# Transform pieces ahead of the layers: a Fourier mixing and a two-layer network woven into one stream of matmuls

## The chip, the cores and the metric

One core of a Trainium2 chip runs the whole kernel in one launch. The metric is the time of the launch on the device, in microseconds; the time given for a kernel is the median of its runs.

## The reference

```python
def _attn_ref(x, filt_r, filt_i):            # x: (8, 3008, 256), filters: (1505, 256)
    X = np.fft.rfft(x, axis=1)
    F = (filt_r + 1j * filt_i)[None, :, :]
    Y = X * F
    return np.fft.irfft(Y, n=x.shape[1], axis=1).astype(np.float32)

def _moe_ref(x, w_in, w_out, alpha):         # x: (24064, 256), w_in: (256, 2048), w_out: (2048, 256)
    h = x @ w_in
    g = np.maximum(h, 0.0) + alpha * np.minimum(h, 0.0)
    return (g @ w_out).astype(np.float32)
```

Each of 8 batches of 3008 tokens is filtered along its tokens in the frequency domain, and all 24064 tokens then go through two layers with a leaky step between them.

## The kernel before

The Fourier transform of length 3008 is split into 47 x 64 and done with small matrices, in stages that the code calls pieces. `piece_a` is the first stage (16 pieces a batch): a matmul of 512 columns on `xs`, which ScalarE moves out of the accumulator into `asb`. `save_a` writes a quarter of `asb` to memory, and `turn_a` reads it back with the axes exchanged into `at`. `piece_b` is a forward pair (12 a batch): two matmuls, and two VectorE products with the filter, `ww` and `uu`, that read the accumulator; GpSimd then sends `ww` with its halves exchanged to `sw` by two transfers. `piece_s` adds `sw` to `uu` on VectorE. `piece_c` is the inverse stage (12): matmuls on `uu`, moved out to `v` by ScalarE; in the batch of index 1 there is no `piece_s`, and `piece_c` takes four matmuls, on `uu` and `sw`. `turn_c` writes `v` to memory and, after the last quarter, reads `zt` back. `piece_d` is the last stage (16): four small matmuls on `zt`, moved out to `yT`, which the layers read.

Batch 0 is done by a class of its own, `First`, ahead of everything; its last 12 turns (`piece_t`) and last-stage pieces are left for the first steps of the layers.

The layers run over 48 blocks of tokens (512 each, one in twelve of 384). A block has 16 steps. In step j, `up(j)` multiplies 128 columns of the first weights with the block's tokens (two matmuls, L414); in odd steps ScalarE moves two steps' results together to `gtb` (L420), and VectorE applies the leaky step (two L423, one L424). `down(j)` does a sixteenth of the second layer of the block before (four matmuls, L433); at its steps 7 and 15 ScalarE moves a result to `osb` (L438), and SyncE's queue stores it.

The order on each engine is the order in which the program is written. A dictionary, `plan`, holds for each step a list of pieces, put there by `put(step, fn, *args)`. In the main loop a step writes `up(j)`, then `down(j)` of the block before, then the pieces of that step in the order in which they were put. Six blocks, 96 steps, pass while one batch goes through the layers; `plan_fft` spreads the pieces of batch index b over the steps before its tokens are needed. Its arguments are the step of the first `piece_a` and their spacing (`a0`, `ga`), the step of `turn_a` (`ta`), the first `piece_b` and the spacing (`b0`, `gap`), the distance to `piece_s` and `piece_c` (`add`, `lag`), and the first `piece_d` (`d0`). A batch's first stage overlaps the forward and inverse stages of the batch before it.

The accumulator memory has 8 banks: the layers' first results `hps` take two buffers of two banks, the second layer's `op` two, and all transform pieces share the last two, the buffers `psF`. A piece can start when one of these two has been emptied, by ScalarE (a, c, d), or by VectorE's two products (b).

Of the kernel before, what the change touches and what calls it, by code (L numbers as in the profile page):

```python
# [64 lines left out]
def kernel(  # L65
# [59 lines left out]
    def load_x(b, c):  # L125
        xs = p_x.tile([2 * N1, 8 * D], FP16, name="xs")
        for h in range(2):
            nc.gpsimd.dma_start(out=xs[h * N1 : h * N1 + N1], in_=xrow(b, h, c))  # L128
        return xs
# [113 lines left out]
    both = (on_act, on_dve)  # L243
# [198 lines left out]
    plan = {}  # L442

    def put(step, fn, *args):
        plan.setdefault(step, []).append((fn, args))

    def plan_fft(b, a0, ga, ta, b0, gap, add, lag, d0, quarters=1, x_late=False):
        f = Fft(b)
        for i in range(16):
            put(a0 + ga * i, f.piece_a, i, on_act)  # L450
        for c in range(4):
            put(a0 + ga * (4 * c + 3), f.save_a, c)
            if b + 1 < NB:
                put(int(b0 + gap * c) + 1 if x_late else a0 + ga * (4 * c + 3) + 1,
                    lambda b=b, c=c: xc.update({(b + 1, c): load_x(b + 1, c)}))
        for q in range(quarters):
            w = NK1 // quarters
            put(ta, f.turn_a, nc.sync, w * q, w * q + w)
        for kp in range(12):
            put(int(b0 + gap * kp), f.piece_b, kp)  # L460
            if add:
                put(int(b0 + gap * kp) + add, f.piece_s, kp)
            put(int(b0 + gap * kp) + lag, f.piece_c, kp, on_act)
        for q in range(4):
            put(int(b0 + gap * (3 * q + 2)) + lag + 1, f.turn_c, q)
        for i in range(16):
            put(d0 + min(i, 4) + 2 * max(i - 4, 0), f.piece_d, i, on_act)

    for g, t0, d0, gap, evs in ((1, 0, 4, 1, both), (2, 17, 24, 2, (on_dve,)), (3, 32, 40, 2, (on_act,))):
        for i in range(4):  # L470
            put(t0 + gap * i, f0.piece_t, 4 * g + i, evs[i % len(evs)])
            put(d0 + gap * i, f0.piece_d, 4 * g + i, evs[i % len(evs)])
# [4 lines left out]
    for i in range(4):  # L477
        put(17 + 3 * i, neg, 6 * i, 6 * i + 6)
    put(29, lambda: nc.gpsimd.dma_start(out=filt_s[64:128], in_=filt_s[0:64]))
    plan_fft(1, 16, 1, 32, 44, 2.5, 0, 6, 92, 4)  # L480
    plan_fft(2, 66, 2, 97, 110, 4.5, 8, 13, 187, 4, True)
    for b in range(3, NB):
        p = 96 * (b - 1)
        plan_fft(b, p - 62, 2, p - 27, p + 6, 5, 8, 13, p + 91, 1, True)

    prev = None
    step = 0
    for p, t0, tn, _ in blocks:
        blk = Block(p, t0, tn)
        for j in range(16):  # L490
            blk.up(j)
            if prev is not None:
                prev.down(j)
            for fn, args in plan.pop(step, ()):
                fn(*args)
            step += 1
        prev = blk
    for q in range(16):
# [32 lines left out]
```

## Time and profile before

| | |
|---|---|
| median of 3 runs | 805.74 us (804.57 to 806.27) |
| the profiled execution's own time | 805.14 us |
| its span, first to last instruction | 803.4 us |
| TensorE matmuls busy | 779.2 us (97%) |
| TensorE weight loads busy | 539.9 us (67%) |
| VectorE busy | 646.5 us (80%) |
| ScalarE busy | 595.6 us (74%) |
| GpSimd busy | 139.9 us (17%) |
| moved by transfers | 100.59 MB, 125 GB/s on average |
| granted TensorE clock | 0.999 |

The times of the runs are of the whole launch; the span is that of one profiled execution. Matmuls overlap in the records, so a busy TensorE need not be one at full speed: the distance from one start to the next tells that. A bracket behind a row of the timeline is the time in which the engine stood idle just before it, and what ended that.

### The profile page before, as it was taken

Reading aid. Unit: us, or ns where it says so; the run is one execution under the profiler, and the core shown is the slowest. Engines: PE = TensorE matmul, PEld = TensorE weight load, DVE = VectorE, ACT = ScalarE, POOL = GpSimd, SP = SyncE. Lnnn points to the kernel's source line nnn. Section 1 sums busy time; section 2 is a strip of 40 time slices with the busy share of each in tenths; the row PEclk is TensorE's granted clock in tenths of the full one; section 3 lists DMA queues with packets and bytes.
Section 4 is the critical chain, followed back from the end, with each engine's and each line's share of the span. In section 5 each row is a group of like instructions: output and inputs, shape, how many; then the busy total and the mean of one; then the engine's idle time right before and its main releaser. Section 6 shows DMA issues by size and latency. Waiting matters only on the chain.

```text
span 803.4 us, 16151 instructions
## 1 busy us (share of the span) xinstructions
PE 779.2 (97%) x5980; PEld 539.9 (67%) x5980; DVE 646.5 (80%) x1449; ACT 595.6 (74%) x836; POOL 139.9 (17%) x269
## 2 busy tenths in 40 slices
PE   6989999999999999999999999999999999999997
PEld 5756667666667666776667766766666766776665
DVE  4797886698878987798877988789877899777773
ACT  3677668878777787777867787687877776686663
POOL 7511230042103210041201321032100122000000
PEclk9999999999999999999999999999999999999999
DMA  9968546474574447464483644845475134511111
GB/s 182 209 135 186 138 109 201 140 155 127 142 180 102 109 112 184 138 119 125 118 198 91 142 115 118 215 93 112 112 180 143 47 89 103 135 40 31 40 40 53
DMA packets 94247, 100.59 MB, mean 125 GB/s; under 512 B 11320, under 2 KB 81992, under 8 KB 94040
## 3 DMA queue, kind: packets, MB, share of 16 engines
q1 hardware_dynamic: 79512, 68.80, 31.8%
q0 software_dynamic: 14656, 30.75, 20.1%
q8 instruction: 47, 0.77, 0.4%
q14 instruction: 32, 0.26, 0.1%
HBM read 56.26 MB, written 46.66 MB: 128 GB/s over the span
## 4 chain that ended last, share of the span: by engine, by line
PE 88%; DVE 6%; ACT 4%; issue 1%; DMA 1%; POOL 0%; ACTq 0%; DVEq 0%; POOLq 0%
PE op L433 38%; PE hps L414 37%; PE psF L164 3%; PE psF L231 3%; PE psF L209 2%; PE psF L184 2%; ACT gtb L420 2%; DVE gtb L424 2%; DVE m L423 1%; DMA xs<-in_x_dram 1%; DVE ww L188 1%; DVE uu L189 1%; PE hps L281 1%; ACT v L238 1%; ACT osb L438 0%
## 5 line engine op out<-in xcount | busy, mean ns | idle before, releaser
L420 ACT ACTIVATE gtb<-hps 128x1024 f16<-128x1024 f32 (+1 forms) x384 | 384.9, 1003 | 115.1 <-PE hps L414 113.9
L433 PE MATMUL op<-wout_s,gtb 128*128 128x256 f16 x3008 | 451.1, 272 | 0.6 <-DVE gtb L424 0.6
L414 PE MATMUL hps<-yT,win_s 128*128 128x512 f16 (+1 forms) x1536 | 449.5, 374 | 1.9 <-ACT yT L238 1.5
L433 PEld LDWEIGHTS <-gtb 128*128 128x128 f16 x3008 | 293.2, 98 | 190.8 <-DVE m L423 1.4
L423 DVE TENSOR_SCALAR m<-gtb,alm_s 128x512 f16<-128x512 f16 (+1 forms) x768 | 237.7, 351 | 108.4 <-ACT gtb L420 107.0
L424 DVE TENSOR_TENSOR gtb<-gtb,m 128x1024 f16<-128x1024 f16 (+1 forms) x384 | 261.6, 681 | 22.7
L191 POOL DMA_DIRECT2D sw<-ww x168 | 87.7, 527 | 499.1 <-DVE ww L188 488.2
L414 PEld LDWEIGHTS <-win_s 128*128 128x128 f16 x1536 | 145.4, 98 | 34.0 <-issue 6.2
L238 ACT ACTIVATE asb<-psF 96x512 f16<-96x512 f32 x112 | 66.4, 593 | 34.6 <-PE psF L164 33.9
L238 ACT ACTIVATE yT<-psF 128x376 f16<-128x376 f32 x120 | 58.0, 483 | 10.7 <-PE psF L231 10.6
L238 ACT ACTIVATE v<-psF 128x512 f16<-128x512 f32 x84 | 50.1, 596 | 16.5 <-PE psF L209 16.4
L438 ACT ACTIVATE osb<-op 128x512 f32<-128x512 f32 x96 | 56.1, 584 | 6.1 <-issue 3.2
L188 DVE TENSOR_TENSOR ww<-psF,filts_s 128x512 f16<-128x512 f32 x84 | 57.4, 684 | 0.3 <-PE psF L184 0.3
L189 DVE TENSOR_TENSOR uu<-psF,filt_s 128x512 f16<-128x512 f32 x84 | 57.2, 681 | 0.0
L164 PE MATMUL psF<-xs,wf_s 94*96 94x512 f16 x112 | 43.2, 386 | 5.9 <-ACT v L238 2.7
L231 PE MATMUL psF<-wi_s,zt 96*128 96x94 f16 x504 | 42.1, 204 | 1.8 <-DVE zt L241 1.2
L128 POOL DMA_DIRECT2D xs<-in_x_dram x64 | 34.4, 547 | 35.5 <-PE psF L164 23.2
L231 PEld LDWEIGHTS <-zt 96*128 96x128 f16 x512 | 35.6, 97 | 6.5 <-issue 2.0
L209 PE MATMUL psF<-uu,twi_s 128*128 128x256 f16 x168 | 33.4, 273 | 0.0
L184 PE MATMUL psF<-at,twf_s 128*128 128x256 f16 x168 | 32.1, 272 | 1.1 <-ACT yT L238 0.9
L196 DVE TENSOR_TENSOR uu<-uu,sw 128x512 f16<-128x512 f16 x72 | 30.1, 418 | 0.0
L209 PEld LDWEIGHTS <-twi_s 128*128 128x128 f16 x192 | 18.5, 98 | 2.1
(57 smaller groups left out, 192.5 us busy)
## 6 DMA issues: line engine op xcount, KB each, us to landing
out_dram<-osb SPq DMA_DIRECT2D x128, 128.0 KB
xs<-in_x_dram POOLq DMA_DIRECT2D x64, 188.0 KB, 4.6
a_dram<-asb SPq DMA_DIRECT2D x28, 384.0 KB
sw<-ww POOLq DMA_DIRECT2D x168, 64.0 KB, 2.1
v_dram<-v SPq DMA_DIRECT2D x112, 96.0 KB
zt<-v_dram SPq DMA_DIRECT2D x28, 384.0 KB
at<-a_dram SPq DMA_DIRECT2D x20, 384.0 KB
at<-a_dram SPq DMA_DIRECT2D x32, 96.0 KB
```

What stands on the lines that cost most here:

```text
L164: nc.tensor.matmul(ps[0:96], wf1_s, xs[:, o : o + 512], start=True, stop=True)
L188: nc.vector.tensor_mul(ww, px, filts_s[:, 2 * kp : 2 * kp + 2])
L189: nc.vector.tensor_mul(uu, px, filt_s[:, 2 * kp : 2 * kp + 2])
L191: nc.gpsimd.dma_start(out=sw[o : o + 64], in_=ww[64 - o : 128 - o])
L209: nc.tensor.matmul(pv[:, kh], twi_s[:, k1], u[:, kh], start=u is us[0], stop=u is us[-1])
L231: nc.tensor.matmul(ps[:, m], self.zt[:, 8 * g + 4 * mh + m, dh * 128 : dh * 128 + 128], wi3_s, start=True, stop=True)
L238: nc.scalar.activation(o, i, AF.Copy)
L414: nc.tensor.matmul(self.hps[:, j % 2, 0:tn], win_s[:, kt, j * 128 : (j + 1) * 128], yT[:, kt, self.t0 : self.t0 + tn], start=(kt == 0), st ...
L420: nc.scalar.activation(g[:, :, 0:tn], self.hps[:, :, 0:tn], AF.Copy)
L423: nc.vector.tensor_scalar(m[:, i, 0:tn], g[:, i, 0:tn], 0.0, a, OP.min, OP.mult)
L424: nc.vector.tensor_add(g[:, :, 0:tn], g[:, :, 0:tn], m[:, :, 0:tn])
L433: nc.tensor.matmul(self.op[:, si % 2], self.gts[k][:, 128 * si : 128 * si + 128], wout_s[:, k], start=(k == 0), stop=(k == 15))
```

## The change

Four things change, all in the order of the same instructions.

1. In each step the pieces are written ahead of `up(j)` and `down(j)`, not behind them.
2. `piece_b` is put at `b0` plus an even number wherever `piece_s` is used (index 2 on), and `b0` is odd there: `p + 5` in place of `p + 6`, 109 in place of 110. So these forward pairs stand in odd steps; `piece_s`, `piece_c` and `turn_c` follow at the old distances.
3. From index 3 on the first stage begins at `p - 70` with a spacing of 2.5 steps, 40 steps in all; it began at `p - 62` with a spacing of 2.
4. The steps of the loads of the next batch's x are given as a list. For the batch of index 2 (the third) the last two of the four loads move from steps 28 and 32 to 73 and 74.

Besides, the last-stage pieces of batch 0 that begin at steps 4 and 24 begin at 6 and 25.

```diff
-    def plan_fft(b, a0, ga, ta, b0, gap, add, lag, d0, quarters=1, x_late=False):
+    def plan_fft(b, a0, ga, ta, b0, gap, add, lag, d0, quarters, x_at):
         f = Fft(b)
         for i in range(16):
-            put(a0 + ga * i, f.piece_a, i, on_act)
+            put(int(a0 + ga * i), f.piece_a, i, on_act)
         for c in range(4):
-            put(a0 + ga * (4 * c + 3), f.save_a, c)
+            put(int(a0 + ga * (4 * c + 3)), f.save_a, c)
             if b + 1 < NB:
-                put(int(b0 + gap * c) + 1 if x_late else a0 + ga * (4 * c + 3) + 1,
+                put(x_at[c],
                     lambda b=b, c=c: xc.update({(b + 1, c): load_x(b + 1, c)}))
...
+        bs = [b0 + (2 * int(gap * kp / 2) if add else int(gap * kp)) for kp in range(12)]
         for kp in range(12):
-            put(int(b0 + gap * kp), f.piece_b, kp)
+            put(bs[kp], f.piece_b, kp)
             if add:
-                put(int(b0 + gap * kp) + add, f.piece_s, kp)
-            put(int(b0 + gap * kp) + lag, f.piece_c, kp, on_act)
+                put(bs[kp] + add, f.piece_s, kp)
+            put(bs[kp] + lag, f.piece_c, kp, on_act)
         for q in range(4):
-            put(int(b0 + gap * (3 * q + 2)) + lag + 1, f.turn_c, q)
+            put(bs[3 * q + 2] + lag + 1, f.turn_c, q)
...
-    for g, t0, d0, gap, evs in ((1, 0, 4, 1, both), (2, 17, 24, 2, (on_dve,)), (3, 32, 40, 2, (on_act,))):
+    for g, t0, d0, gap, evs in ((1, 0, 6, 1, both), (2, 17, 25, 2, (on_dve,)), (3, 32, 40, 2, (on_act,))):
...
-    plan_fft(1, 16, 1, 32, 44, 2.5, 0, 6, 92, 4)
-    plan_fft(2, 66, 2, 97, 110, 4.5, 8, 13, 187, 4, True)
+    plan_fft(1, 16, 1, 32, 44, 2.5, 0, 6, 92, 4, (20, 24, 73, 74))
+    plan_fft(2, 66, 2, 97, 109, 4.5, 8, 13, 187, 4, (110, 114, 118, 122))
     for b in range(3, NB):
         p = 96 * (b - 1)
-        plan_fft(b, p - 62, 2, p - 27, p + 6, 5, 8, 13, p + 91, 1, True)
+        plan_fft(b, p - 70, 2.5, p - 27, p + 5, 5, 8, 13, p + 91, 1, (p + 6, p + 10, p + 16, p + 20))
...
         for j in range(16):
+            for fn, args in plan.pop(step, ()):
+                fn(*args)
             blk.up(j)
             if prev is not None:
                 prev.down(j)
-            for fn, args in plan.pop(step, ()):
-                fn(*args)
             step += 1
```

## The prediction

> **What bounds the kernel now.** I read the page first, then the timeline of TensorE, then the waits of single stretches, then VectorE and ScalarE around each wait.
>
> ```profile
> span 803.4 us, 16151 instructions
> PE 779.2 (97%) x5980; PEld 539.9 (67%) x5980; DVE 646.5 (80%) x1449; ACT 595.6 (74%) x836; POOL 139.9 (17%) x269
> ```
>
> TensorE is the bound by its busy share. Whether that busy time is also full speed is read from the starts:
>
> ```profile
> 401.10 0.59 PE L414 MATMUL hps<-yT,win_s 128*128 128x512 f16 x2
> 401.53 0.60 PE L433 MATMUL op<-wout_s,gtb 128*128 128x256 f16 x4
> 401.96 0.59 PE L414 MATMUL hps<-yT,win_s 128*128 128x512 f16 x2
> ```
>
> Two matmuls of 512 columns take 0.43 us, four of 256 columns 0.43 us: a step is 0.87 us, and outside a few places every step in the timeline has just this length. The order of matmuls can win nothing there. What is left to win are the places where TensorE stands. After the first block those taken up below come to some 12 us, and nearly all are of one kind: a transform piece waits for one of the two psF banks. The timeline of one such place, the last of its window (two rows), and the row of the waits of 352 to 420 us:
>
> ```profile
> 363.68 0.38 PE L184 MATMUL psF<-at,twf_s 128*128 128x256 f16 x2
> 364.50 0.61 DVE L423 TENSOR_SCALAR m<-gtb,alm_s 128x512 f16<-128x512 f16 x2 [0.16 <-ACT gtb L420]
> 365.75 0.68 DVE L188 TENSOR_TENSOR ww<-psF,filts_s 128x512 f16<-128x512 f32 x1
> 366.36 0.68 DVE L189 TENSOR_TENSOR uu<-psF,filt_s 128x512 f16<-128x512 f32 x1
> 366.50 0.38 PE L209 MATMUL psF<-uu,twi_s 128*128 128x256 f16 x2
> 367.09 0.42 PE L164 MATMUL psF<-xs,wf_s 94*96 94x512 f16 x1 [0.21 <-DVE uu L189]
> 367.35 0.38 PE L414 MATMUL hps<-yT,win_s 128*128 128x512 f16 x1
> 399.55 0.38 PE L209 MATMUL psF<-uu,twi_s 128*128 128x256 f16 x2
> 400.23 0.60 PE L414 MATMUL hps<-yT,win_s 128*128 128x512 f16 x2
> ```
>
> ```profile
> PEld L164 <- DVE uu L189: 1.6, 4, 0.5
> ```
>
> The forward pair (L184) of an odd step ends up behind that step's own layer pair on VectorE: the pair's L423 starts at 364.50, ww only at 365.75, and the bank is free at 367.04, 3.36 us after its matmuls began. Three steps on an inverse piece (L209) takes the other bank, and the first-stage piece (L164) of the next batch stands. From c to the next layer matmul should be 0.43 us and is 0.85: 0.42 lost, twice what the bracket says. Each window in which two batches overlap has four such places (the row of the waits; the last is 399.55 to 400.23, 0.24 lost); two cost 0.42 and two 0.24, **1.3 us a window**, and there are four windows (batch indices 3 to 6).
>
> That was a pair of an odd step. One of an even step stands behind the same VectorE work but starts a step later, so it holds its bank for less time:
>
> ```profile
> 369.08 0.38 PE L184 MATMUL psF<-at,twf_s 128*128 128x256 f16 x2
> 370.94 0.68 DVE L189 TENSOR_TENSOR uu<-psF,filt_s 128x512 f16<-128x512 f32 x1
> ```
>
> That is 2.54 us to 371.62. Which bank a piece gets is not strictly alternating; I take the one that is free first.
>
> **What the change is, in positions.** Pieces of step s written before up(s) stand where those of step s-1 stood: all move one step earlier, except where a start was raised too (d0 of the first two groups). So parity turns over. New odd pieces stand like old even ones: a forward pair holds its bank 2.5 us, and a ScalarE eviction starts at once. New even pieces stand like old odd ones: a forward pair holds 3.36 us, and a ScalarE eviction queues behind the layer's own:
>
> ```profile
> 361.48 1.02 ACT L420 ACTIVATE gtb<-hps 128x1024 f16<-128x1024 f32 x1 [0.71 <-PE hps L414]
> 361.72 0.38 PE L209 MATMUL psF<-uu,twi_s 128*128 128x256 f16 x2
> 361.94 0.59 PE L414 MATMUL hps<-yT,win_s 128*128 128x512 f16 x2
> 362.40 0.59 ACT L238 ACTIVATE v<-psF 128x512 f16<-128x512 f32 x1
> 372.35 0.38 PE L209 MATMUL psF<-uu,twi_s 128*128 128x256 f16 x2
> 373.07 0.59 ACT L438 ACTIVATE osb<-op 128x512 f32<-128x512 f32 x1
> 373.55 0.60 ACT L238 ACTIVATE v<-psF 128x512 f16<-128x512 f32 x1
> ```
>
> Such an inverse piece frees its bank 1.27 us after it starts (362.99), and 1.80 us where the output eviction of steps 7 and 15 of a block comes between (374.15). A piece itself takes 0.22 us of TensorE (361.72 to 361.94). No matmul, eviction or transfer is added or dropped.
>
> **Windows of indices 3 to 6.** With p = 96(b-1) as in the code, forward pairs now stand at p+5, 9, 15, 19, 25, 29, ..., inverse pieces at p+18, 22, 28, 32, 38, ..., first-stage pieces of the next batch at p+26, 28, 31, 33, 36, 38, .... The place of the old wait is three steps behind a pair: 3 x 0.87 and a piece are 2.8 us, past 2.5, so those four waits go: gain 1.3. What is late next is a pair one step behind an inverse and a first-stage piece (28 to 29, 38 to 39, 48 to 49, 58 to 59): it comes 2 x 0.22 + 0.87 = 1.31 us after c, whose bank is free at 1.27. That is 0.03 each with the time of a signal, but at 48 the output eviction is in between: 1.80 - 1.31 and the signal, 0.55. At 18 to 19 it is 0.07. Together 0.7, so **0.6 us gained in each of four windows, 2.5 in all**, and 0.1 lost in the last batch, which had no wait.
>
> **Index 2, steps 122 to 159.** Its old waits are three of this kind, the first being
>
> ```profile
> 179.54 0.38 PE L164 MATMUL psF<-xs,wf_s 94*96 94x512 f16 x1 [0.47 <-ACT v L238]
> 144.30 0.38 PE L414 MATMUL hps<-yT,win_s 128*128 128x512 f16 x1 [1.09 <-ACT yT L238]
> ```
>
> at 0.6 lost each, with small ones 2.0. New: at 121 a pair, at 122 an inverse and a first-stage piece; the latter comes 1.3 us after the pair and finds both banks held till 2.4: 1.1 lost. At 145 and 153 a pair stands behind an inverse piece behind an output eviction: 0.5 each. Four small ones 0.5. That is 2.6: **0.65 lost**. The second row is the layer at step 96 that waits for the transform piece just ahead of it; with the piece a step earlier 0.87 us of work lies between, and its eviction, now in an odd step, starts at once: **1.0 gained**.
>
> **Index 1, steps 44 to 72.**
>
> ```profile
> 85.68 0.13 PEld L184 LDWEIGHTS <-twf_s 128*128 128x128 f16 x2 [1.00 <-DMA at<-a_dram]
> 116.72 0.38 PE L164 MATMUL psF<-xs,wf_s 94*96 94x512 f16 x1 [0.68 <-ACT v L238]
> ```
>
> The wait for the turned data goes if the two moved x loads leave the transfer engines earlier to it. But the pair at 44 is then in an even step of the new kind and holds 3.36 us, and the next pair at 46, two steps and two pieces on (2.2 us), stands 1.2: no gain, 0.2 lost. At 66 a first-stage piece comes 2.6 us behind the even pair of 64: 0.7 against nothing before. At 70 and 72 (the second row is the first of the two, about 0.64 lost each) it comes 1.5 us behind an odd pair that holds 2.5 and just behind an inverse piece that now waits for the layer's eviction: 0.95 each. That is 0.2 + 0.7 + 0.6: **1.5 lost**; bounds 0 (both banks free where I count them held at 46 and 66) and 2.2.
>
> The moved loads are issued at 73 and 74 on POOL behind the last swap:
>
> ```profile
> 117.80 0.38 PE L184 MATMUL psF<-at,twf_s 128*128 128x256 f16 x2
> 120.91 0.52 POOL L191 DMA_DIRECT2D sw<-ww  x1 [2.42 <-DVE ww L188]
> xs<-in_x_dram POOLq DMA_DIRECT2D x64, 188.0 KB, 4.6
> ```
>
> The swap is issued 3.1 us after the pair of step 71; two swaps and two loads at 0.52 each and 4.6 to land make 9.8 us, and the first user is step 82, 11 steps or 9.6 us and some 3 us of pieces later. Cost nothing; without that cover up to 3 us.
>
> **The first block and steps 16 to 31.**
>
> ```profile
> 41.66 0.68 DVE L241 CAST zt<-psF 96x512 f16<-96x512 f32 x1
> 42.39 0.33 PE L231 MATMUL psF<-wi_s,zt 96*128 96x94 f16 x4 [0.48 <-DVE zt L241]
> 45.66 0.33 PE L231 MATMUL psF<-wi_s,zt 96*128 96x94 f16 x4
> 50.10 0.59 PE L414 MATMUL hps<-yT,win_s 128*128 128x512 f16 x2 [0.20 <-ACT gtb L420]
> 55.34 0.38 PE L164 MATMUL psF<-xs,wf_s 94*96 94x512 f16 x1 [0.30 <-DVE zt L241]
> 61.91 0.33 PE L231 MATMUL psF<-wi_s,zt 96*128 96x94 f16 x4 [0.24 <-ACT asb L238]
> 62.91 0.38 PE L164 MATMUL psF<-xs,wf_s 94*96 94x512 f16 x1 [0.67 <-DVE zt L241]
> ```
>
> The second turn's eviction now stands ahead of the first layer pair on VectorE, not behind it (41.66), and starts near 38.8. ScalarE then takes layer pair 0 at 39.3, a turn at 40.2, pairs 1 and 2 to 41.8 and 42.7 and the first transform piece to 43.1. So these pieces run at about 41.5, 42.4, 43.1 and, by the bank it gets, 44.6 or 45.3, against 42.39 to 45.66. From the last one to step 16 it took 4.4 us for eight layer steps; with one step fewer 4.0. Step 16 starts at 48.6 to 49.3, not 50.10: **1.2 gained**. Later the three waits, bracketed 0.30, 0.24, 0.67 and some 1.7 in starts, go, since turn and first-stage pieces part; what comes is a first-stage piece behind the last layer evictions of block 0 (0.3) and two short ones (0.4): **1.0 gained**; bounds of both together 0.5 and 2.6.
>
> **The sum**: 2.5 - 0.1 - 0.65 + 1.0 - 1.5 + 1.2 + 1.0 = 3.45 us off the profiled run's 805.14 us (span 803.4, 1.7 around it): 801.7. The median of the runs shown, 805.74, lies 0.6 above the profiled one, so I forecast a median of **802.3 us**.
>
> **Rivals.**
> - *The waits only change place* (chance 0.14). Two banks stay two banks; at x8 to x9 the margin is 0.04 us. If each window keeps its 1.3 us, the sum falls by 2.5 to 0.95: 804.8 by the median. For it: the wait at 48 exists by my own count. Against: 2.5 us held instead of 3.36 clears the old places by 0.3. The Trainium skill, "Perfetto Trace Analysis", "Optimization Strategy", reads a gap that keeps repeating as too few buffers, which would be this case.
> - *VectorE is the real bound, no change* (0.04). In a window, five steps give VectorE 2.5 layer pairs of 1.25 us (364.50 to 365.75), one forward pair of 1.3 and one add of some 0.4: 4.8 us. TensorE needs 5 x 0.87 and four pieces, 5.2. If its work were shorter than 4.8, shorter bank waits would uncover VectorE and the time stay at 805.7. The rows at 401 speak against it: 215 ns for each 512-column matmul leaves TensorE the longer by 0.4. The Trainium skill, "TensorE: Matmul & The Clock Gate", "Back-to-back issue gap", gives 131 ns for it in a stream with weight loads; by that the rival would hold, and the trace does not agree.
> - *Inverse evictions come late, slower* (0.10). All inverse pieces of indices 2 to 7 now stand in even steps, behind the layer eviction. Besides those counted, 20 pairs stand one step behind one (four in each window, three in index 2, one in the last batch). If ScalarE is late at each by 0.3 us more, half of one more eviction of 0.59, 20 x 0.3 = 6.0 are lost: 808.3. It turns slower past 3.45 / 20 = 0.17 us each. Against: ScalarE is 74% busy, and nothing else stands between in the order.
> - *More* (0.14). The pair at 46 and the piece at 122 find a bank, and the start gives 0.4 more (its upper bound): 1.2 + 1.1 + 0.4, 799.6.
> - That nothing changes because the shift is only one of labels would need the starts raised by one everywhere; the diff raises two.
>
> **How the numbers follow.** The forecast has 0.58. About 0.2% (1.6 us) is what a measurement can tell from no change. Faster takes the forecast and "more", 0.72; same takes "change place" and VectorE, 0.18; slower 0.10. The bounds (start 0.5 to 2.6, index 1 from 0 to -2.2) and these cases give 799.4 to 805.2.
>
> **What would show it.** The waits of L164 for uu in the four windows gone; L184 waiting for v once a window, at p+49, about 0.5 us; step 16 at 48.6 to 49.3 us; the wait of L414 for yT at step 96 gone; a wait of L184 at step 46 near 1 us. It is wrong if L184 waits for v at each x9, or if L164 waits for xs at step 82.

## The result, and the profile after

| | before | after |
|---|---|---|
| median of 6 runs each | 805.88 us (804.57 to 807.98) | 800.07 us (798.82 to 801.05) |
| ratio, 95% interval | | 0.9925 (0.9909 to 0.9941) |
| the profiled execution's own time | 805.14 us | 799.77 us |
| its span | 803.4 us | 798.0 us |

The change makes the kernel 0.75% faster, 5.8 us by the medians and 5.4 by the profiled executions. The forecast was 3.45 us, to 802.3; the result lies inside the range (799.4 to 805.2), near its lower end.

The head of the page after, which answers to that of before:

```profile
span 798.0 us, 16169 instructions
PE 778.0 (97%) x5980; PEld 542.0 (68%) x5980; DVE 646.1 (81%) x1449; ACT 597.9 (75%) x836; POOL 140.6 (18%) x269
```

The counts of the matmuls, of VectorE's and of ScalarE's operations are those of before, and their busy times moved by less than 0.5%. So no work was saved; TensorE stands less. TensorE's waits in the two kernels from 50 to 800 us (what waited, for what; total us, times, longest), first before:

```profile
PE psF L164 <- ACT v L238: 2.7, 5, 0.7
PE psF L164 <- DVE uu L189: 1.9, 8, 0.3
PE hps L414 <- ACT yT L238: 1.1, 1, 1.1
PE psF L164 <- DVE zt L241: 1.0, 2, 0.7
...
```

and then after:

```profile
PE psF L184 <- ACT v L238: 2.1, 6, 0.3
PE psF L164 <- DVE uu L189: 1.3, 2, 0.7
PE psF L184 <- DVE uu L189: 1.0, 1, 1.0
PE psF L164 <- DMA xs<-in_x_dram: 0.9, 1, 0.9
...
```

First-stage pieces (L164) no longer wait eight times for a forward pair's products, nor for the last turns (`zt`); the layer no longer waits for `yT`. In their place stand six waits of a forward pair (L184) for an inverse piece's eviction `v`, and a few single ones. The totals are too small: in the place shown next the bracket says 0.35 us where the starts show 0.51 lost. So I use the starts from here on: **lost time** is the distance between two layer starts less the time that the step's matmuls take where nothing waits (for instance 0.87 us a step of 512 tokens, 0.22 us a piece of 512 columns, 0.43 for an inverse piece of index 1 with its four matmuls). One of the six, as the timeline after shows it:

```profile
377.58 1.02 ACT L420 ACTIVATE gtb<-hps 128x1024 f16<-128x1024 f32 x1 [0.45 <-PE hps L414]
377.82 0.38 PE L209 MATMUL psF<-uu,twi_s 128*128 128x256 f16 x2
378.04 0.38 PE L164 MATMUL psF<-xs,wf_s 94*96 94x512 f16 x1
378.50 0.59 ACT L438 ACTIVATE osb<-op 128x512 f32<-128x512 f32 x1
378.98 0.60 ACT L238 ACTIVATE v<-psF 128x512 f16<-128x512 f32 x1
379.64 0.38 PE L184 MATMUL psF<-at,twf_s 128*128 128x256 f16 x2 [0.35 <-ACT v L238]
```

This is step p+48 with its pair at p+49. The inverse piece starts at 377.82; its eviction stands behind the layer's (`gtb`) and the output's (`osb`), and ends at 379.58. The pair comes 1.60 us behind the first-stage piece where 0.22 + 0.87 = 1.09 would do: 0.51 lost, where the bracket says 0.35. It is the wait that the prediction put at this place with 0.55.

### The profile page after: what moved, and what is told of

Its sections match the earlier page's. It is cut to its first block, busy times and chain, and to the rows that moved or that the text cites. A ratio compares the mean times of both kernels' runs of the same rounds, so it can differ in the third digit from the quotient of the medians.

```text
span 798.0 us, 16169 instructions
## 1 busy us (share of the span) xinstructions
PE 778.0 (97%) x5980; PEld 542.0 (68%) x5980; DVE 646.1 (81%) x1449; ACT 597.9 (75%) x836; POOL 140.6 (18%) x269
## 4 chain that ended last, share of the span: by engine, by line
PE 87%; ACT 4%; DVE 3%; DMA 3%; issue 2%; SPq 1%; POOL 1%; ACTq 0%; DVEq 0%; POOLq 0%
PE op L433 38%; PE hps L414 37%; PE psF L164 3%; PE psF L231 3%; PE psF L184 2%; PE psF L209 2%; ACT gtb L420 2%; DMA xs<-in_x_dram 1%; DMA a_dram<-asb 1%; DVE ww L188 1%; ACT osb L438 1%; DVE m L423 1%; PE hps L281 1%; DVE uu L189 1%; ACT asb L238 1%
## 5 line engine op out<-in xcount | busy, mean ns | idle before, releaser
L414 PE MATMUL hps<-yT,win_s 128*128 128x512 f16 (+1 forms) x1536 | 449.1, 374 | 0.4 <-ACT gtb L420 0.2
L414 PEld LDWEIGHTS <-win_s 128*128 128x128 f16 x1536 | 145.0, 98 | 31.9 <-issue 4.0
L164 PE MATMUL psF<-xs,wf_s 94*96 94x512 f16 x112 | 42.7, 381 | 3.0 <-DVE uu L189 1.3
L184 PE MATMUL psF<-at,twf_s 128*128 128x256 f16 x168 | 32.0, 272 | 3.0 <-ACT v L238 2.1
```

The source lines that it names most:

```text
L164: nc.tensor.matmul(ps[0:96], wf1_s, xs[:, o : o + 512], start=True, stop=True)
L414: nc.tensor.matmul(self.hps[:, j % 2, 0:tn], win_s[:, kt, j * 128 : (j + 1) * 128], yT[:, kt, self.t0 : self.t0 + tn], start=(kt == 0), st ...
```

## The experiments

All were timed beside the kernel before on the same chip. Four undo or isolate a part of the change; the other four follow from what these showed. The lost time after step 16, counted in the same way in every trace:

| kernel | median, us | ratio to before (95%) | lost after step 16, us | median less lost |
|---|---|---|---|---|
| before | 805.88 | | 14.35 | 791.5 |
| after | 800.07 | 0.9925 (0.9909 to 0.9941) | 10.03 | 790.0 |
| e1, order alone | 801.39 | 0.9943 (0.9924 to 0.9963) | 11.80 | 789.6 |
| e2, pairs in even steps | 810.60 | 1.0056 (1.0036 to 1.0076) | 20.58 | 790.0 |
| e3, x loads early | 799.29 | 0.9922 (0.9896 to 0.9949) | 10.04 | 789.3 |
| e4, old spread | 800.44 | 0.9932 (0.9911 to 0.9953) | 11.12 | 789.3 |
| e5, output eviction later | 796.09 | 0.9878 (0.9864 to 0.9892) | 6.93 | 789.2 |
| e6, other places | 796.02 | 0.9878 (0.9866 to 0.9891) | 6.31 | 789.7 |
| e7, both | 792.53 | 0.9838 (0.9822 to 0.9854) | 3.19 | 789.3 |
| e8, the changed kernel again | 800.31 | 0.9933 (0.9919 to 0.9946) | 10.54 | 789.8 |

The last column tells whether the lost time explains the times: with the pieces ahead of the layers it is 789.2 to 790.0 for kernels 18 us apart, so it does, to about 1 us. Before stands 1.5 us above the changed kernel: the fourth column leaves out the first block, where before is slower by about as much.

### e1: the order alone

```diff
         for j in range(16):
+            for fn, args in plan.pop(step, ()):
+                fn(*args)
             blk.up(j)
             if prev is not None:
                 prev.down(j)
-            for fn, args in plan.pop(step, ()):
-                fn(*args)
             step += 1
```

> The order of before with one edit: the pieces are written ahead of up and down, all starts and spacings as before. Theory (a piece waits for one of two psF banks; how long a bank is held goes by the parity of its step): the parity of every piece turns over, so in each window the four old waits go but others come (an inverse piece one step behind a first-stage piece of an even step, 0.2 each, 0.7 behind the output eviction at 48): about 1.15 us a window against 1.3. Step 96 gains 1.4, the first block about 1.0, the rest 0.5: 802.4 us. Rival (the order alone makes the gain): 800. Rival (the new starts and spacings make it): 805 or more.

Measured 801.39 us, 1.0 below what I expected: point 1 of the change alone gives 0.57 of the 0.75% (the intervals overlap). The forward pairs stand alternately in odd and even steps here, as before. The largest waits from 50 to 800 us:

```profile
PE psF L164 <- ACT v L238: 1.4, 2, 0.7
PE psF L164 <- DVE uu L189: 1.3, 2, 0.7
PE psF L184 <- DMA at<-a_dram: 1.3, 1, 1.3
PE psF L209 <- DVE uu L189: 1.1, 2, 0.5
```

The windows lost 0.80, 1.21, 0.79 and 1.23 us, less than the 1.3 to 1.4 of before and more than the 0.65 of after. The lost time at step 96 is 0.04, as after, and step 44 loses 1.43 us, waiting for turned data. The first block shows what the two raised starts of batch 0 are worth: from the first layer matmul to step 16 it takes 12.23 us before, 11.31 here and 10.77 after, so 0.9 of that gain is the order and 0.5 the starts raised from 4 to 6 (the other raised start lies behind step 16).

### e2: the pairs of index 2 to 7 in even steps

```diff
-    plan_fft(2, 66, 2, 97, 109, 4.5, 8, 13, 187, 4, (110, 114, 118, 122))
+    plan_fft(2, 66, 2, 97, 108, 4.5, 8, 13, 187, 4, (110, 114, 118, 122))
-        plan_fft(b, p - 70, 2.5, p - 27, p + 5, 5, ...
+        plan_fft(b, p - 70, 2.5, p - 27, p + 4, 5, ...
```

> The changed kernel with the forward pairs of index 2 on one step earlier, so in even steps. Theory: such a pair holds its bank 3.36 us, not 2.5, and the first-stage piece three steps on waits again (0.35 each), some others 0.2: about 1.6 us a window against 0.66, less 0.5 in index 2: 803.3 us. Rival (the parity does not matter): 800.1.

Measured 810.60 us, 10.5 slower than the change and 4.7 slower than before: the sign of the theory, but more than twice the size. The windows lost 2.70, 3.34, 2.69 and 3.34 us. What the expectation left out are the inverse pieces. One place, from the timeline of this kernel:

```profile
358.84 0.38 PE L164 MATMUL psF<-xs,wf_s 94*96 94x512 f16 x1
359.53 0.58 ACT L238 ACTIVATE asb<-psF 96x512 f16<-96x512 f32 x1
359.57 0.68 DVE L189 TENSOR_TENSOR uu<-psF,filt_s 128x512 f16<-128x512 f32 x1
360.16 0.38 PE L209 MATMUL psF<-uu,twi_s 128*128 128x256 f16 x2
```

The pair three steps before the inverse piece began at 356.89 and holds its bank until 360.25, and the first-stage piece in the other bank is moved out at 360.11. The inverse piece starts at 360.16, 1.32 us behind the first-stage piece where 1.09 would do: 0.23 lost, here and at the like places (0.22 to 0.43), with up to 0.93 at p+17. So a pair that holds 3.36 us in place of 2.5 can delay an inverse piece too, not only the next first-stage piece. The hold itself goes by parity in every trace: from a pair's first matmul to the end of its `uu`, in the 60 pairs of indices 3 to 7, it is 2.4 to 3.0 us in even steps and 3.2 to 3.6 in odd ones before; after, all are in odd steps with 1.8 to 2.9; here, all are in even steps with 3.4 to 3.8. The edit also moves the inverse pieces, which follow their pairs, against the first stage of the next batch; how much of the 10.5 us is that, no run separates.

### e3: x for the third batch early

```diff
-    plan_fft(1, 16, 1, 32, 44, 2.5, 0, 6, 92, 4, (20, 24, 73, 74))
+    plan_fft(1, 16, 1, 32, 44, 2.5, 0, 6, 92, 4, (20, 24, 28, 32))
```

> The changed kernel with the two moved loads back at steps 28 and 32. Theory: the pair of step 44 waits again for the turned data, some 1 us, and the pair of 46, which waits 1.13 us for its bank in the changed kernel, then finds it free: no change within 0.3, 800.1 us. Rival (the later loads are worth the whole wait): 801.1.

Measured 799.29 us; the lost time is that of the changed kernel, 10.04 against 10.03. The wait for turned data that I expected back at 44 did not come. The first row is the issue of the turned reads in this kernel, the second its first pair, then the same two in the changed kernel and in e1, each from its own timeline:

```profile
77.91 8.48 SPq L176 DMA_DIRECT2D at<-a_dram  x16
81.74 0.38 PE L184 MATMUL psF<-at,twf_s 128*128 128x256 f16 x2
```

```profile
74.13 7.61 SPq L176 DMA_DIRECT2D at<-a_dram  x16
82.33 0.38 PE L184 MATMUL psF<-at,twf_s 128*128 128x256 f16 x2
```

```profile
79.53 8.68 SPq L176 DMA_DIRECT2D at<-a_dram  x16
83.17 0.38 PE L184 MATMUL psF<-at,twf_s 128*128 128x256 f16 x2 [1.27 <-DMA at<-a_dram]
```

In e1 the pair starts 3.64 us after the issue, as soon as its data is there; in e3 it comes 3.83 us after, so it just finds its data, with 0.2 to spare; in the changed kernel it comes 8.20 after. So the later loads let the turn start earlier, by 3.8 us in the two traces and by 4.4 counted from the first pair, which here only buys margin. What makes the turn of e1 1.6 us later than that of e3, with the same loads, no run settles: the two differ in several places ahead of it. Nor was it run whether the moved loads alone would take away e1's wait.

### e4: the old spread of the first stage

```diff
-        plan_fft(b, p - 70, 2.5, p - 27, p + 5, 5, ...
+        plan_fft(b, p - 62, 2, p - 27, p + 5, 5, ...
```

> The changed kernel with the first stage of index 3 on over 32 steps again (from p - 62, every 2 steps). Theory: no bank is held longer for it; in the windows the same one wait of 0.5 at p+49 and small ones, 0.66 us; in index 2 the first piece moves away from the pair of step 121 and its wait of 1.11 goes, with 0.3 more: 798.7 us. Rival (spreading the first stage relieves ScalarE and VectorE, and that is the gain in the windows): 1.3 us a window again, 802.7.

Measured 800.44 us against 800.07, no difference beyond the intervals. The theory was right on the windows: 0.65, 0.64, 0.64 and 0.62 us lost, with either spread. It was wrong on index 2. The wait at 122 went, as said, and two others of 1.1 us came at 140 and 158, where a first-stage piece now stands one step behind a pair and just behind an inverse piece. The first of them, from the timeline of this kernel:

```profile
181.57 0.38 PE L184 MATMUL psF<-at,twf_s 128*128 128x256 f16 x2
182.66 0.38 PE L209 MATMUL psF<-uu,twi_s 128*128 128x256 f16 x2
183.34 0.59 ACT L238 ACTIVATE v<-psF 128x512 f16<-128x512 f32 x1
183.99 0.38 PE L164 MATMUL psF<-xs,wf_s 94*96 94x512 f16 x1 [0.94 <-ACT v L238]
```

This is the pattern (pair in s, inverse and first-stage piece in s+1) that costs 1.11 us: one time in the changed kernel, two times here. I had applied the rule to one place only. Index 2 loses 0.8 more in this trace than after; a further 0.4 is lost at step 60, where an inverse piece waits for its swap (see e8).

### e5: the output eviction behind the next step's pieces

If the six waits for `v` come from `osb` standing ahead of it on ScalarE, it is enough to write `osb` later.

```diff
...
-                    osb = p_osb.tile([128, 2, D], FP32, name="osb")
-                    nc.scalar.activation(osb[:, 0:m], self.op[:, 0:m], AF.Copy)
-                    for lane in range(m):
-                        store(self.p, self.t0 + 128 * (si - m + 1 + lane), osb, lane)
+                    def give(op=self.op, m=m, t=self.t0 + 128 * (si - m + 1)):
+                        osb = p_osb.tile([128, 2, D], FP32, name="osb")
+                        nc.scalar.activation(osb[:, 0:m], op[:, 0:m], AF.Copy)
+                        for lane in range(m):
+                            store(self.p, t + 128 * lane, osb, lane)
+                    late.append(give)
...
             for fn, args in plan.pop(step, ()):
                 fn(*args)
+            while late:
+                late.pop(0)()
             blk.up(j)
...
```

> The changed kernel with the output evictions of steps 7 and 15 of a block written behind the pieces of the next step, not ahead of them. Theory: the waits of 0.5 us at p+49 in four windows, at 145 and 153, and of 0.44 at 24 are an inverse or first-stage eviction queued behind an output eviction on ScalarE; all go, 3.4 us: 796.7 us. Rival (ScalarE is loaded there and the wait only moves to another place): 800.1.

Measured 796.09 us, 4.2 less than the changed kernel on the same chip (e8); the seven expected places (steps 25, 145, 153 and p+49 in four windows) lose 0.49 us less each than in the first trace of the changed kernel, 3.4 in all, as expected. From the timeline of this kernel, a place where the changed one waits:

```profile
284.56 0.38 PE L209 MATMUL psF<-uu,twi_s 128*128 128x256 f16 x2
285.25 0.59 ACT L238 ACTIVATE v<-psF 128x512 f16<-128x512 f32 x1
285.89 0.38 PE L184 MATMUL psF<-at,twf_s 128*128 128x256 f16 x2
286.20 0.60 ACT L440 ACTIVATE osb<-op 128x512 f32<-128x512 f32 x1
```

`v` ends at 285.84, 1.28 us after its piece began, and the pair starts without a bracket. All waits of L184 for `v` are gone from its view of waits, the windows lose 0.15 to 0.23 us. `osb` itself comes later; no row of TensorE's waits names it, only the store on SyncE's queue waits for it, as before.

### e6: other places for what still waits

The pair at 46, the first-stage pieces of index 2 and the one at 122 stand badly by the same rule; here they stand in other steps.

```diff
-    for g, t0, d0, gap, evs in (... (3, 32, 40, 2, (on_act,))):
+    for g, t0, d0, gap, evs in (... (3, 32, 41, 1, (on_act,))):
-    plan_fft(1, 16, 1, 32, 44, 2.5, 0, 6, 92, 4, (20, 24, 73, 74))
-    plan_fft(2, 66, 2, 97, 109, 4.5, 8, 13, 187, 4, (110, 114, 118, 122))
+    plan_fft(1, 16, 1, 32, 43, 2.5, 0, 6, 92, 4, (20, 24, 73, 74))
+    plan_fft(2, 72, 1.6, 97, 109, 4.5, 8, 13, 187, 4, (110, 114, 118, 122))
-        plan_fft(b, p - 70, 2.5, p - 27, p + 5, 5, ...
+        plan_fft(b, p - 68, 2.25 if b == 3 else 2.5, p - 27, p + 5, 5, ...
```

> The changed kernel with three places changed, nothing taken away: the forward pairs of index 1 from step 43 and the four last-stage pieces of batch 0 ahead of them in steps 41 to 44; the first stage of index 2 from step 72 every 1.6 steps; that of index 3 from 124 every 2.25 and of the later ones from p - 68 every 2.5. Theory: a wait is only a matter of who holds the two banks, so counting holds of 2.5 and 3.36 (pairs) and 1.27 and 1.80 us (ScalarE) shows where none is left: the waits of 1.13 at 46, 0.8 at 66, 0.9 and 0.28 at 70 and 72 and of 1.11 at 122 and 0.28 at 159 go, and 0.2 comes at 65: 795.7 us. Rival (index 1 is short of VectorE time, so its waits return elsewhere): 798 or more. If the turned data are not there at 43, up to 1 us more.

Measured 796.02 us, lost 6.31. The wait at 46 fell to 0.09 us (its pair now stands at 45), index 2 to 1.20; at 65 and 76 there are 0.38 and 0.22 left.

### e7: both

The edits of e5 and e6 together.

> The edits of the two kernels above together. Theory: the savings add, 3.4 and 4.4, and one overlap of 0.4 at 153 goes with them: about 792 us, with some 2.2 us of waits left after step 16, most of it before step 32. Rival (another engine becomes the bound once the waits are gone): 795 or more.

Measured 792.53 us, 7.8 us below the changed kernel on the same chip and 13.3 below the kernel before: the fastest version here. The head of its page and TensorE's waits from 50 to 800 us:

```profile
span 791.3 us, 16155 instructions
PE 776.5 (98%) x5980; PEld 542.0 (68%) x5980; DVE 644.9 (81%) x1449; ACT 596.5 (75%) x836; POOL 140.6 (18%) x269
```

```profile
PE psF L209 <- DMA sw<-ww: 0.6, 1, 0.6
PE op L434 <- DVE gtb L425: 0.6, 1, 0.6
```

No wait for a bank of psF is left in this view. One inverse piece, at step 76, waits for its swap (0.8 us lost by the starts), which the expectation did not have, and the last block waits for the leaky step. The lost time is 3.19 us where 2.2 was expected. The two parts nearly add: 4.2 and 4.3 us alone, 7.8 together.

### e8: the changed kernel beside them

> The changed kernel itself, on the same chip as the three above: 800.1 us.

Measured 800.31 us, which agrees with the first runs of the changed kernel (800.07). The trace has 10.54 us lost where the first had 10.03. The difference is one place: at step 60 an inverse piece of index 1 waits for its swap, 0.51 us by the starts, where the first trace shows no wait:

```profile
PE psF L209 <- DMA sw<-ww: 0.3, 1, 0.3
```

The same place loses 0.25 to 0.54 us in e1, e2, e4 and e5, and nothing in e3. Why the swap comes later in some executions, the runs do not show.

## Why the prediction came out as it did

The sign and the mechanism (who holds the two banks, and for how long) were right; the sum was 1.9 us short of the profiled 5.37, and nearly all of that is one term, index 1, while the misses of the other terms nearly cancel. Its terms, in us gained, against the lost time in the two traces:

| term | predicted | lost before | lost after | gained |
|---|---|---|---|---|
| four windows, index 3 to 6 | 2.5 | 1.44, 1.33, 1.36, 1.32 | 0.67, 0.64, 0.67, 0.64 | 2.8 |
| last batch | -0.1 | 0 | 0.06 | -0.1 |
| index 2, steps 121 to 164 | -0.65 | 1.97 | 2.53 | -0.56 |
| step 96, with the steps 81 to 120 around it | 1.0 | 1.50 | 0.04 | 1.46 |
| index 1, steps 44 to 80 | -1.5 | 3.42 | 3.18 | 0.24 |
| first block | 1.2 | step 16 at 50.10 us | at 49.26 us, one piece (0.22) further | 1.06 |
| steps 16 to 31 | 1.0 | 2.11 | 1.71 | 0.4 |
| sum | 3.45 | | | 5.3 |

**Windows.** As worked out: waits of L164 for `uu` gone, one of L184 for `v` left at p+49 (0.51 against 0.55). The waits from 348 to 416 us after, where before had four of 1.6 in all:

```profile
PE psF L184 <- ACT v L238: 0.3, 1, 0.3
```

e4 shows that the spread over 40 steps has no part in it, e1 and e2 that order and the steps of the pairs have.

**Index 2.** The three places at 122, 145 and 153 were the right ones: 1.11, 0.51 and 0.51 lost, where 1.1, 0.5 and 0.5 were predicted. The first, after:

```profile
163.80 0.38 PE L184 MATMUL psF<-at,twf_s 128*128 128x256 f16 x2
164.89 0.38 PE L209 MATMUL psF<-uu,twi_s 128*128 128x256 f16 x2
165.57 0.59 ACT L238 ACTIVATE v<-psF 128x512 f16<-128x512 f32 x1
166.22 0.38 PE L164 MATMUL psF<-xs,wf_s 94*96 94x512 f16 x1 [0.94 <-DMA xs<-in_x_dram]
```

The bracket names the load of x, but `v` ends at 166.16 and frees the bank for 166.22. The prediction said that it would be wrong if L164 waited for xs at step 82; this one is at 122, and in e3 and e8 the same wait is put down to `v`.

**Index 1: the step that failed.** I predicted 1.5 us lost; 0.24 was gained (by e8's trace, with the wait for the swap at 60, 0.3 lost). The wait at 46 came as said, 1.13 lost. Three sizes were off. The old waits at 70 and 72 had cost 0.85 each, not 0.64. At 56 I had a small old wait (0.37) uncounted that went away. And the new wait at 72 is 0.28 us, not 0.95:

```profile
114.68 0.42 PE L164 MATMUL psF<-xs,wf_s 94*96 94x512 f16 x1 [0.70 <-DVE uu L189]
115.80 0.38 PE L184 MATMUL psF<-at,twf_s 128*128 128x256 f16 x2
116.22 0.69 DVE L188 TENSOR_TENSOR ww<-psF,filts_s 128x512 f16<-128x512 f32 x1 [0.30 <-PE psF L184]
116.83 0.68 DVE L189 TENSOR_TENSOR uu<-psF,filt_s 128x512 f16<-128x512 f32 x1
117.56 0.42 PE L164 MATMUL psF<-xs,wf_s 94*96 94x512 f16 x1
```

While TensorE stood 0.90 us at step 70, VectorE went on with its queue: at 116.22 it waits for the pair (0.30), and the pair's bank is free 1.71 us after its start, at 117.51, not after 2.5. I had priced both waits from the same hold of 2.5 us, as if the first left the second unchanged. That it is the first wait that shortens the second is read from these rows; no run takes the first away and leaves the second.

**Step 96 and the start.** The wait of L414 for `yT` went; I had taken 1.0 for it. By the starts it had cost 1.25 where its bracket said 1.09 (the second layer matmul of the step came 1.47 us behind the first, where 0.22 would do), and 0.2 more was lost two steps ahead of it. After, the eviction (140.36 to 140.84) ends 0.5 us ahead of the layer that reads it:

```profile
140.00 0.33 PE L231 MATMUL psF<-wi_s,zt 96*128 96x94 f16 x4
140.36 0.48 ACT L238 ACTIVATE yT<-psF 128x376 f16<-128x376 f32 x1
141.31 0.60 PE L414 MATMUL hps<-yT,win_s 128*128 128x512 f16 x2
```

The first layer matmul and that of step 16, after:

```profile
38.50 0.61 PE L414 MATMUL hps<-yT,win_s 128*128 128x512 f16 x2
49.26 0.59 PE L414 MATMUL hps<-yT,win_s 128*128 128x512 f16 x2
```

Step 16 is inside the predicted 48.6 to 49.3, but that is partly luck: in the nine traces with the pieces first it lies between 48.16 and 49.44. The first layer matmul, now with the pieces of step 0 ahead of it, came 0.6 us later than before:

```profile
37.87 0.61 PE L414 MATMUL hps<-yT,win_s 128*128 128x512 f16 x2 [0.41 <-ACT yT L238]
```

From the first to step 16 the gain is (50.10 - 37.87) - (49.26 - 38.50) = 1.47; the 0.63 by which the first mark came later, from the pieces ahead of it or by chance, goes off this. Steps 16 to 31 gave 0.4 where I took 1.0: the three old waits went, but 0.2 to 0.3 came at 17, 19 and 21, and 0.60 at 25 behind an `osb` that I had not placed there (in e5 it is 0.10).

**The rivals.** *Change place*: half of it, as predicted, not all; e7 shows that two banks are enough if the evictions stand right. The Trainium skill, "Perfetto Trace Analysis", "Optimization Strategy", says that a gap that keeps repeating can mean too few buffers; here the lost time fell from 14.35 us to 3.19 with the same two. *VectorE the real bound*: out; at 81% it let the time fall to 792.53. *Inverse evictions late, slower*: out, with the places behind `osb` as its grain of truth; the other three pairs of a window lose some 0.15 in all, not 0.3 each. *More* came nearest in time (799.6), but not by its reasons: the pair at 46 (1.13) and the piece at 122 (1.11) both waited.

## What to carry to other kernels

When many kinds of work share two buffers, write down for each how long it holds one at its place in the evicting engine's queue (here 1.27 or 1.80, 2.5 or 3.36 us), and go through every place by that list, not only those that wait now. Put evictions that no matmul is waiting for behind those that free a shared buffer: here both are as long as each other (0.59 us), and that alone gave 4.2 us by the medians. Price waits by the distance of starts, not by their brackets, and one after the other: a wait can give the evicting engine time to catch up, as at steps 70 and 72 here, so that two near ones need not add.

## What was not expected of the hardware

The first layer matmul starts at 37.36 to 38.67 us in the ten traces, and among the nine with the pieces first, all with the same order ahead of it, the range is the same: 38.50 and 38.65 in the two traces of the changed kernel, 37.90 in e3, 37.36 in e4. So what lies ahead of the layers moves by up to 1.3 us from one trace to another, as much as a term of the sum, and such terms are to be compared by starts inside their stage. Inside the layers the one place that differs like this is the swap at step 60: 0.51 us lost in one trace of the changed kernel and nothing in the other.
